# Summing the residual and the skip product in SBUF with an accumulating DMA, in a kernel that adds a state-space layer and a gated feed-forward layer

## The chip, the cores and the metric

The kernel runs on one core of one Trainium2 chip. The metric is device time in microseconds of one execution; the median of three runs of the kernel before is 177.08 us (176.98 to 179.34). The engines of the core are named as in the profile: PE (matrix products), DVE (vector), ACT (scalar), POOL (GpSimd) and SP, whose queue issues most DMAs.

## The reference

The input x has 2048 rows of 512 features. It is normalized once (xn), and three things are added to x: a diagonal complex state-space layer over the 2048 rows, a skip product xn * Dskip, and a GELU-gated feed-forward layer with 1376 hidden features.

```python
def _A_ref(x, Lambda_re, Lambda_im, B_re, B_im, C_re, C_im, log_dt, Dskip):
    ...
    Bu = jnp.einsum("bld,pd->blp", x + 0j, B_bar)
    for t in range(L):
        h = Lam_bar[None, :] * h + Bu[:, t, :]
        hs.append(h)
    hseq = jnp.stack(hs, 1)
    return 2.0 * jnp.einsum("blp,dp->bld", hseq, Cmat).real + x * Dskip[None, None, :]

def _B_ref(x, w_gate, w_up, w_down):
    return (_gelu(x @ w_gate) * (x @ w_up)) @ w_down

xn = _layernorm(x, axis=-1)
return x + _A_ref(xn, ...) + _B_ref(xn, ...)
```

The normalization of a row, (x - mean) / sqrt(var + eps), has no learned scale. All tensors are bfloat16, and so is the output.

## The kernel before

The 2048 rows are cut into four blocks of 512 rows, and each block into four tiles of 128 rows, so that there are 16 tiles. X holds all 16 input tiles in SBUF. XN holds normalized tiles in a ring of eight: tile tt lies in slot tt % 8, so block 2 overwrites the slots of block 0, and block 3 those of block 1. XD holds the 16 skip products.

For a block b the stages are these.

- LN(b) computes statistics (DVE, L614 and L615), a root on POOL (L621) and the normalized tiles (DVE, L633). For block 3 this is LN_act(3): mean and sum of squares on ACT (L652, L654), which also writes its by-product into the XN slots, then the root (POOL, L658) and the normalized tiles (DVE, L663).
- TR(b) transposes the four normalized tiles into XNT with four DMAs on SP's queue (L735).
- SKIP(b) multiplies each normalized tile with Dskip into XD, four products on DVE (L670).
- GU(b) multiplies with the gate and up weights (PE, L842), eleven tiles of hidden features. ACT evacuates the gate with the GELU (L857) and the up product (L861), DVE multiplies them (L863). The eleventh, of 96 features, goes another way (L816, L823, L825, L826) and needs a transposing DMA on SP (L828). For block 0 the first seven are computed in another way at the start of the kernel (L700, L711), and H0_T transposes them by DMA (L729).
- BU(b) is the input product of the state-space layer (PE, L748; evacuated by ACT, L757). CHAIN(b) is its recurrence on DVE: a rotation (L773 to L779), eight scans (L786), a carry for the next block and a rotation back (L798 to L802). scale_C scales the output matrix once (ACT, L591; DVE, L594).
- DN(b) forms the output of each tile in one PSUM bank. seed(j) writes X into the bank (ACT, L875); hidden(j) adds the eleven products with w_down, states(j) the eight products of the state-space layer (PE, L883, none of which starts a new sum); store(j) adds XD on DVE while it evacuates the bank into OUTB (L901), and a DMA on SP writes it out (L903). In blocks 0 and 1 all four hidden parts come ahead of the four states parts. Block 3 is the tail: its last tile is cut in columns, 384 and 128, in two banks.

PSUM has eight banks, which are taken in a ring in the order of the program. A tile of GU takes two, the eleventh tile two, a unit of BU one, DN four (the tail one more).

The order of the work comes from a planner inside the kernel. The program states its operations in a sequence with their reads and writes. PE and SP keep that sequence. On DVE, ACT and POOL the planner orders by due time: it goes back from the operations that need a result, with assumed durations, and picks, of what is ready, what is due first, filling gaps with later work. For a DMA it assumes 2 us plus its bytes at 350 bytes per ns. The order is fixed when the program is built, so on the chip an engine that waits for one operation also holds up all that stand behind it. Waits are semaphores, one for each DMA and one for each engine.

The sequence around the change, from the main part of build():

```python
CHAIN(1)
LN(2); SKIP(2)
TR(2)
load_C()
late_loads()
scale_C()
GU(1, [0, 1, 2, 10, 3, 4, 5, 6, 7, 8, 9])
BU(2)
CHAIN(2)
DN(0, True)
LN_act(3); SKIP(3)
GU(2, [0, 1, 2, 10, 3, 4, 5, 6, 7]); TR(3); GU(2, [8, 9])
```

Of the kernel before, what the change touches and what calls it, by code (L numbers as in the profile page):

```python
# [9 lines left out]
ALU = mybir.AluOpType  # L10
ACTF = mybir.ActivationFunctionType
BF16, F32, I32 = dt.bfloat16, dt.float32, dt.int32
# [333 lines left out]
L, D, P, F = 2048, 512, 512, 1376  # L346
NT, NB, KD, KP, KF = 16, 4, 4, 4, 11
# [17 lines left out]
def build(nc, ins, out):  # L365
    with ExitStack() as es:
        E = es.enter_context
        S = Sched(nc, es)
        ARENA_BYTES = 207 * 1024
        arena_t = E(nc.sbuf_tensor("arena", [128, ARENA_BYTES // 2], BF16))  # L370
        A = Arena(arena_t, ARENA_BYTES)
        PS = [E(nc.psum_tensor("PS%d" % i, [128, 512], F32)) for i in range(8)]
        BANK = [Buf("bank%d" % i, "ps", i, i + 1) for i in range(8)]

        def ring(parent, name, n):
            return [A.sub(parent, "%s%d" % (name, i), i) for i in range(n)]
# [10 lines left out]
        WDc = [Buf("WDc%d" % i, "sbx", 200 + 10 * i, 201 + 10 * i) for i in range(2)]  # L387
        XNT_all = A.alloc("XNT", [NB, KD, TB_], BF16)
        XNT = ring(XNT_all, "XNT", NB)
        X_all = A.alloc("X", [NT, D], BF16)  # L390
        X = ring(X_all, "X", NT)
        XN_all = A.alloc("XN", [8, D], BF16)
        XN = ring(XN_all, "XN", 8)
        DSKB = A.alloc("DSKB", [D], BF16)
        XD_all = A.alloc("XD", [NT, D], BF16); XD = ring(XD_all, "XD", NT)
        IDN = A.alloc("IDN", [128], BF16)
        BBT_all = A.alloc("BBT", [2, KD, P], BF16)
        BBT = [[A.sub(A.sub(BBT_all, "BBTc%d" % c, c), "BBT%d_%d" % (c, k), k) for k in range(KD)] for c in range(2)]
# [1 line left out]
        CT = [[A.sub(A.sub(CT_all, "CTc%d" % c, c), "CT%d_%d" % (c, s), s) for s in range(KP)] for c in range(2)]  # L400
# [57 lines left out]
        HTt = [[A.sub(HT[k], "HT%d_%d" % (k, ft), ft) for ft in range(KF)] for k in range(2)]  # L458
        SSs = [[A.sub(SSb[k], "SS%d_%d" % (k, s), s) for s in range(KP)] for k in range(3)]
# [4 lines left out]
        V = lambda fn, dur, r, w, tag="", after=(): S.op("vector", fn, dur, r, w, tag, after)  # L464
        ACT = lambda fn, dur, r, w, tag="", after=(): S.op("scalar", fn, dur, r, w, tag, after)
        POOL = lambda fn, dur, r, w, tag="", after=(): S.op("gpsimd", fn, dur, r, w, tag, after)
        PE = lambda fn, dur, r, w, tag="": S.op("tensor", fn, dur, r, w, tag)
# [70 lines left out]
        def load_C():  # L538
            load_T(CRAW, ("A_C_re", "A_C_im"))
# [85 lines left out]
        def recip(qb, rq):  # L625
            return V(lambda e: e.reciprocal(rq.ap, qb.ap), 150, [qb], [rq], "rq")
# [11 lines left out]
        def LN(b, js=range(4)):  # L638
            for j in js:
                stats(b, j)  # L640
            _, mn, qb, rq = root(b, js[0], js[-1] + 1)
            recip(qb, rq)
            norms(b, js, mn, rq, js[0])
# [4 lines left out]
        def LN_act(b):  # L648
            for j in range(4):
                tt = 4 * b + j  # L650
                xs = XN[tt % 8]
                ACT(lambda e, j=j, tt=tt, xs=xs: e.activation(xs.ap, X[tt].ap, ACTF.Copy, scale=-1.0 / D, accum_out=NMBs[j].ap),  # L652
                    d_act(512) + 190, [X[tt]], [xs, NMBs[j]], "mean")
                ACT(lambda e, j=j, tt=tt, xs=xs: e.activation(xs.ap, X[tt].ap, ACTF.Square, bias=NMBs[j].ap, accum_out=SQBs[j].ap),  # L654
                    d_act(512) + 190, [X[tt], NMBs[j]], [xs, SQBs[j]], "sq")
            sbq, qb, rq = (cols(t, b, 0, 4) for t in (SBQ, QB, RQ))
            V(lambda e: e.tensor_scalar(sbq.ap, SQB.ap, 1.0 / D, EPS_BF16, ALU.mult, ALU.add), D_TINY, [SQB], [sbq], "sbq")
            POOL(lambda e: e.tensor_tensor(qb.ap, sbq.ap, HALF.ap, ALU.pow), 1100, [sbq, HALF], [qb], "pow")  # L658
            recip(qb, rq)
            last = None  # L660
            for j in range(4):
                tt = 4 * b + j
                last = S.order_behind(V(lambda e, j=j, tt=tt: e.tensor_scalar(  # L663
                    XN[tt % 8].ap, X[tt].ap, NMBs[j].ap, rq.ap[:, j:j + 1], ALU.add, ALU.mult),
                    d_dve_ts4x(512), [X[tt], NMBs[j], rq], [XN[tt % 8]], "ln_n"), last)

        def SKIP(b):
            for tt in range(4 * b, 4 * b + 4):
                xs = XN[tt % 8]
                V(lambda e, tt=tt, xs=xs: e.tensor_tensor(XD[tt].ap, xs.ap, DSKB.ap, ALU.mult),  # L670
                  d_dve_tt2x(512), [xs, DSKB], [XD[tt]], "skip")

        XCd = lambda j, k: XC_all.ap[:, k, 128 * j:128 * (j + 1)]

# [57 lines left out]
        def TR(b, js=range(4)):  # L732
            for j in js:
                tt = 4 * b + j
                S.dma(lambda e, b=b, j=j, tt=tt: e.dma_start_transpose(  # L735
                    XNT[b].ap[:, :, 128 * j:128 * (j + 1)], XN[tt % 8].ap),
                    1.6 * 128 * 1024, reads=[XN[tt % 8]], writes=[XTk[b][j]], tag="tr_x%d" % b, issue=1280.0)
# [129 lines left out]
        def DN(b, split=False, tail=None):  # L867
            k2, k3 = b % 2, b % 3
            banks = [next_bank() for _ in range(4)]
            xbank = next_bank() if tail else None  # L870

            def seed(j, c0=0, c1=D):
                tt, bank = 4 * b + j, banks[j]
                bank = banks[j] if c0 == 0 else xbank
                ACT(lambda e: e.activation(PS[bank][:, c0:c1], X[tt].ap[:, c0:c1], ACTF.Copy), d_act(c1 - c0), [X[tt]], [BANK[bank]], "seed")  # L875

            def mms(j, ops, last, rds, c0, c1):
                bank = banks[j] if c0 == 0 else xbank

                def f(e):  # L880
                    ins_ = None
                    for n, (l_, r_) in enumerate(ops):
                        ins_ = e.matmul(PS[bank][:, c0:c1], l_[:, 128 * j:128 * (j + 1)], r_[:, c0:c1], start=False,  # L883
                                        stop=last and n == len(ops) - 1, skip_group_check=True)
                    return ins_
                PE(f, d_pe([c1 - c0] * len(ops)), rds + [BANK[bank]], [BANK[bank]], "DN%d" % b)

            def hidden(j, c0=0, c1=D):
                ops = [(HTt[k2][ft].ap[0:FROWS[ft], :], WD.ap[0:FROWS[ft], ft, :]) for ft in range(KF)]
                mms(j, ops, False, [HTt[k2][ft] for ft in range(KF)] + WDc, c0, c1)  # L890

            def states(j, c0=0, c1=D):
                ops = [(SSc[k3][s][c].ap, CT[c][s].ap) for s in range(KP) for c in range(2)]
                mms(j, ops, True, [SSs[k3][s] for s in range(KP)] + [CT[c][s] for c in range(2) for s in range(KP)], c0, c1)

            def store(j, c0=0, c1=D):
                tt = 4 * b + j
                bank = banks[j] if c0 == 0 else xbank
                ko = tt % 4
                ob = OUTB[ko] if c1 - c0 == D else Buf("OUTBp%d" % c0, "sb", OUTB[ko].lo + 2 * c0, OUTB[ko].lo + 2 * c1)  # L900
                V(lambda e: e.tensor_tensor(OUTB[ko].ap[:, c0:c1], PS[bank][:, c0:c1], XD[tt].ap[:, c0:c1], ALU.add),  # L901
                  d_dve_1x(c1 - c0), [BANK[bank], XD[tt]], [ob], "evO")
                S.dma(lambda e: e.dma_start(out[0, 128 * tt:128 * (tt + 1), c0:c1], OUTB[ko].ap[:, c0:c1]),  # L903
                      256 * (c1 - c0), reads=[ob], is_output=True, tag="st_out")

            if split:
                for j in range(4):
                    seed(j); hidden(j)
                for j in range(4):
                    states(j); store(j)  # L910
            elif tail:
                for j in range(3):
                    seed(j); hidden(j)
                for j in range(3):
                    states(j); store(j)
                parts = ((0, tail), (tail, D))
                for c in parts:
                    seed(3, *c)
                for c in parts:
                    hidden(3, *c); states(3, *c); store(3, *c)  # L920
            else:
                for j in range(4):
                    seed(j); hidden(j); states(j); store(j)
# [106 lines left out]
        BU(1, 4)  # L1030
        coefs()
        CHAIN(1)
        LN(2); SKIP(2)
        TR(2)
        load_C()
        late_loads()
        scale_C()
        GU(1, [0, 1, 2, 10, 3, 4, 5, 6, 7, 8, 9])
        BU(2)
        CHAIN(2)  # L1040
        DN(0, True)
        LN_act(3); SKIP(3)
        GU(2, [0, 1, 2, 10, 3, 4, 5, 6, 7]); TR(3); GU(2, [8, 9])
        BU(3)
        CHAIN(3)
        DN(1, True)
# [60 lines left out]
```

## Time and profile before

| | us |
|---|---|
| median of the runs shown | 177.08 (176.98 to 179.34) |
| span of the profiled execution, first to last instruction | 175.8 |
| PE busy | 172.7 (98%) |
| DVE busy | 159.6 (91%) |
| ACT busy | 95.9 (55%) |
| POOL busy | 10.7 (6%) |

The profiled execution is told by its span, 175.8 us; what lies around the span in an unprofiled run is taken as the difference from the median, 1.3 us. The lines of the chain and of a timeline have the start in us, the duration in us, and then the engine, the line of the kernel and the operation with its count; a bracket at the end gives the idle time of the engine just before and what ended it. In the page's list of DMA issues the last number is the median time from issue to landing. A share of busy time is an average over the whole span: it does not tell where an engine was waited for.

### The profile page before, as it was taken

How to read it: one execution, taken by the hardware profiler on the slowest of the kernel's cores; microseconds unless marked ns; L12 is line 12 of the kernel's file. 1: busy time of each engine (PE TensorE's matmuls, PEld its weight loads, DVE VectorE, ACT ScalarE, POOL GpSimd, SP SyncE). 2: the span in 40 equal slices, each digit the busy share in tenths (PEclk: the TensorE clock that was granted, in tenths of full speed). 3: DMA queues.
4: the chain of work that ended last, by engine and by line, in shares of the span. 5: the costliest groups of instructions: out<-in, count | busy, mean ns of one | idle time of the engine just before them, and what ended most of it. 6: DMA issues, size and time to landing. Idle time of an engine off the chain costs nothing.

```text
span 175.8 us, 2521 instructions
## 1 busy us (share of the span) xinstructions
PE 172.7 (98%) x889; PEld 84.7 (48%) x889; DVE 159.6 (91%) x279; ACT 95.9 (55%) x187; POOL 10.7 (6%) x24
## 2 busy tenths in 40 slices
PE   8999999999999999999999999999999999999995
PEld 2545464845544444444644444444454444444453
DVE  5988999997989989889899999989999899999931
ACT  5476678999766898383576792000667960000000
POOL 3212120210000000002100000000000000000000
DMA  5898999794998000002025000002001000000221
GB/s 174 262 323 139 228 158 224 132 138 99 202 306 200 4 0 2 0 30 89 4 45 106 0 0 0 4 0 90 30 0 30 4 0 0 0 0 0 95 95 56
DMA packets 32421, 14.37 MB, mean 82 GB/s; under 512 B 23736, under 2 KB 32408, under 8 KB 32408
## 3 DMA queue, kind: packets, MB, share of 16 engines
q1 hardware_dynamic: 32096, 13.94, 35.1%
q10 hardware_dynamic: 312, 0.27, 0.5%
q8 instruction: 7, 0.11, 0.3%
q14 instruction: 6, 0.05, 0.1%
HBM read 6.46 MB, written 2.10 MB: 49 GB/s over the span
## 4 chain that ended last, share of the span: by engine, by line
PE 96%; DMA 2%; SPq 0%; DVE 0%; issue 0%
PE PS L883 37%; PE PS L842 32%; PE PS L748 16%; PE PS L711 4%; PE PS L816 3%; PE PS L700 3%; DMA arena<-in_B_w_up_dram 2%; PE PS L683 0%; SPq L487 0%; SPq L496 0%; DVE arena L901 0%
## 5 line engine op out<-in xcount | busy, mean ns | idle before, releaser
L883 PE MATMUL PS<-arena 128*128 128x512 bf16 (+3 forms) x323 | 66.2, 366 | 0.0
L842 PE MATMUL PS<-arena 128*128 128x512 bf16 x264 | 58.1, 379 | 0.0
L883 PEld LDWEIGHTS PS<-arena 128*128 128x128 bf16 (+1 forms) x323 | 30.8, 98 | 35.2
L842 PEld LDWEIGHTS PS<-arena 128*128 128x128 bf16 x264 | 25.8, 98 | 30.2
L786 DVE TENSOR_TENSOR_SCAN arena<-arena 128x512 bf16<-128x512 f32 x32 | 38.9, 1254 | 0.0
L857 ACT ACTIVATE arena<-PS 128x512 bf16<-128x512 f32 x33 | 19.8, 599 | 26.1 <-DVE arena L901 16.7
L748 PE MATMUL PS<-arena 128*128 128x512 bf16 (+1 forms) x144 | 28.2, 355 | 0.0
L861 ACT ACTIVATE arena<-PS 128x512 bf16<-128x512 f32 x33 | 19.8, 599 | 5.4 <-PE PS L842 5.4
L748 PEld LDWEIGHTS PS<-arena 128*128 128x128 bf16 x144 | 14.1, 98 | 13.3
L875 ACT ACTIVATE PS<-arena 128x512 f32<-128x512 bf16 (+2 forms) x17 | 9.6, 581 | 19.7 <-DVE arena L901 19.0
L757 ACT ACTIVATE arena<-PS 128x512 bf16<-128x512 f32 x32 | 17.5, 596 | 1.8 <-PE PS L748 1.8
L901 DVE TENSOR_TENSOR arena<-PS,arena 128x512 bf16<-128x512 f32 (+2 forms) x17 | 10.9, 652 | 6.4 <-PE PS L883 6.3
L863 DVE TENSOR_TENSOR arena<-arena 128x512 bf16<-128x512 bf16 x33 | 13.2, 416 | 2.3 <-ACT arena L861 2.2
L775 DVE TENSOR_TENSOR arena<-arena 128x4096 bf16<-128x4096 bf16 (+1 forms) x5 | 9.2, 1858 | 0.4 <-ACT arena L610 0.4
L798 DVE TENSOR_TENSOR arena<-arena 128x4096 bf16<-128x4096 bf16 x4 | 9.1, 2287 | 0.1
L773 DVE TENSOR_TENSOR arena<-arena 128x4096 bf16<-128x4096 bf16 (+1 forms) x5 | 9.2, 1858 | 0.0
L799 DVE TENSOR_TENSOR arena<-arena 128x4096 bf16<-128x4096 bf16 x4 | 9.1, 2284 | 0.0
L720 ACT ACTIVATE arena<-PS,arena 128x256 bf16<-128x256 f32 (+1 forms) x16 | 6.5, 450 | 4.1 <-PE PS L700 2.4
L614 DVE BATCH_NORM_STATS2 arena<-arena 128x6 f32<-128x512 bf16 x12 | 7.7, 681 | 0.0
L711 PE MATMUL PS<-arena 128*128 128x512 bf16 (+1 forms) x40 | 7.1, 336 | 0.0
L723 DVE SCALAR_TENSOR_TENSOR arena<-PS,arena 128x256 bf16<-128x256 f32 (+1 forms) x16 | 6.3, 443 | 0.7 <-PE PS L700 0.7
L700 PE MATMUL PS<-arena 128*128 128x512 bf16 (+1 forms) x30 | 6.1, 342 | 0.3 <-DMA arena<-in_B_w_up_dram 0.3
(95 smaller groups left out, 124.1 us busy)
## 6 DMA issues: line engine op xcount, KB each, us to landing
out_dram<-arena SPq DMA_DIRECT2D x15, 128.0 KB, 1.7
arena<-in_A_x_dram SPq DMA_DIRECT2D x3, 512.0 KB, 5.5
arena<-in_B_w_down_dram SPq DMA_DIRECT2D x1, 1280.0 KB, 7.4
arena<-in_B_w_gate_dram SPq DMA_DIRECT2D x4, 128.0 KB, 3.4
arena<-in_B_w_up_dram SPq DMA_DIRECT2D x4, 128.0 KB, 3.6
arena<-in_B_w_gate_dram SPq DMA_DIRECT2D x1, 480.0 KB, 6.6
arena<-in_B_w_up_dram SPq DMA_DIRECT2D x1, 480.0 KB, 7.4
arena<-arena SPq DMA_TRANSPOSE x25, 3.1
```

Source lines behind the costliest of these rows:

```text
L700: PE(lambda e: e.matmul(dst, XCd(j, k), WGU[:, ws[0]:ws[-1] + 1, k, f0:f1], start=first, stop=k == KD - 1, skip_group_check=True), d_pe([w ...
L711: ins_ = e.matmul(dst, XCd(j, k), WGU[:, :, k, f0:f1], start=(k == 0), stop=(k == KD - 1))
L748: ins_ = e.matmul(PS[bank][:, 128 * j0:128 * j1], BBT[c][dk].ap[:, 128 * s:128 * (s + 1)], XNT[b].ap[:, dk, 128 * j0:128 * j1], start=(dk ...
L757: GATE["evBu"] = ACT(lambda e, bank=bank, k3=k3, s=s, c=c: e.activation(SSc[k3][s][c].ap, PS[bank][:, :], ACTF.Copy), d_act(512), [BANK[ba ...
L786: V(lambda e, g=g, rb=rb, init=init: e.tensor_tensor_scan(g.ap, rb, g.ap, init, ALU.mult, ALU.add), d_dve_scan(512), [g, PA[RRr]] + ([CARc ...
L842: ins_ = e.matmul(PS[bank][0:m, c0:c1], W.ap[:, dk, 128 * ft:128 * ft + m], XNT[b].ap[:, dk, c0:c1], start=(dk == 0), stop=(dk == KD - 1))
L857: GATE["last_gelu"] = ACT(lambda e, bg=bg, kk=kk, m=m: e.activation(GG[kk].ap[0:m, :], PS[bg][0:m, :], ACTF.Gelu_apprx_tanh), d_act(512), ...
L861: ACT(lambda e, bu=bu, kk=kk, m=m: e.activation(UPB[kk].ap[0:m, :], PS[bu][0:m, :], ACTF.Copy), d_act(512), [BANK[bu]], [UPB[kk]], "evU")
L863: V(lambda e, kk=kk, m=m, ft=ft, k2=k2: e.tensor_tensor(HTt[k2][ft].ap[0:m, :], GG[kk].ap[0:m, :], UPB[kk].ap[0:m, :], ALU.mult), d_dve_tt ...
L875: ACT(lambda e: e.activation(PS[bank][:, c0:c1], X[tt].ap[:, c0:c1], ACTF.Copy), d_act(c1 - c0), [X[tt]], [BANK[bank]], "seed")
L883: ins_ = e.matmul(PS[bank][:, c0:c1], l_[:, 128 * j:128 * (j + 1)], r_[:, c0:c1], start=False, stop=last and n == len(ops) - 1, skip_group ...
L901: V(lambda e: e.tensor_tensor(OUTB[ko].ap[:, c0:c1], PS[bank][:, c0:c1], XD[tt].ap[:, c0:c1], ALU.add), d_dve_1x(c1 - c0), [BANK[bank], XD ...
```

## The change

The buffer XD goes away. SKIP(b) now multiplies in place, so that the XN slot holds the skip product, and then one DMA per block, on POOL's queue, adds the block's four XN slots (2048 elements in each partition) into X in SBUF. X then holds x + xn * Dskip. In blocks 0 to 2 ACT seeds the banks with this sum as before, and since nothing is left to add, ACT also evacuates them with a copy. In block 3 there are no seeds: the first product of hidden(j) starts the sum in the bank, and DVE adds X while it evacuates. SKIP(2) and SKIP(3) are stated behind TR(2) and TR(3), which read the same slots.

```diff
-        XD_all = A.alloc("XD", [NT, D], BF16); XD = ring(XD_all, "XD", NT)
...
         def SKIP(b):
             for tt in range(4 * b, 4 * b + 4):
                 xs = XN[tt % 8]
-                V(lambda e, tt=tt, xs=xs: e.tensor_tensor(XD[tt].ap, xs.ap, DSKB.ap, ALU.mult),
-                  d_dve_tt2x(512), [xs, DSKB], [XD[tt]], "skip")
+                V(lambda e, tt=tt, xs=xs: e.tensor_tensor(xs.ap, xs.ap, DSKB.ap, ALU.mult),
+                  d_dve_tt2x(512), [xs, DSKB], [xs], "skip")
+            n0 = (4 * b) % 8
+            S.dma(lambda e, b=b: e.dma_start(X_all.ap[:, 4 * b:4 * b + 4, :], XN_all.ap[:, n0:n0 + 4, :], accum_op=ALU.add),
+                  1024 * 1024, reads=XN[n0:n0 + 4] + X[4 * b:4 * b + 4], writes=X[4 * b:4 * b + 4], tag="acc_x", queue="gpsimd", issue=1200.0)
...
-            def seed(j, c0=0, c1=D):
+            def seed(j):
                 tt, bank = 4 * b + j, banks[j]
-                bank = banks[j] if c0 == 0 else xbank
-                ACT(lambda e: e.activation(PS[bank][:, c0:c1], X[tt].ap[:, c0:c1], ACTF.Copy), d_act(c1 - c0), [X[tt]], [BANK[bank]], "seed")
+                if not tail:
+                    ACT(lambda e: e.activation(PS[bank][:, :], X[tt].ap, ACTF.Copy), d_act(D), [X[tt]], [BANK[bank]], "seed")
...
-                        ins_ = e.matmul(PS[bank][:, c0:c1], l_[:, 128 * j:128 * (j + 1)], r_[:, c0:c1], start=False,
+                        ins_ = e.matmul(PS[bank][:, c0:c1], l_[:, 128 * j:128 * (j + 1)], r_[:, c0:c1], start=first and n == 0,
                                         stop=last and n == len(ops) - 1, skip_group_check=True)
...
-                mms(j, ops, False, [HTt[k2][ft] for ft in range(KF)] + WDc, c0, c1)
+                mms(j, ops, bool(tail), False, [HTt[k2][ft] for ft in range(KF)] + WDc, c0, c1)
...
-                V(lambda e: e.tensor_tensor(OUTB[ko].ap[:, c0:c1], PS[bank][:, c0:c1], XD[tt].ap[:, c0:c1], ALU.add),
-                  d_dve_1x(c1 - c0), [BANK[bank], XD[tt]], [ob], "evO")
+                if not tail:
+                    ACT(lambda e: e.activation(OUTB[ko].ap, PS[bank][:, :], ACTF.Copy), d_act(D), [BANK[bank]], [ob], "evO")
+                else:
+                    V(lambda e: e.tensor_tensor(OUTB[ko].ap[:, c0:c1], PS[bank][:, c0:c1], X[tt].ap[:, c0:c1], ALU.add),
+                      d_dve_1x(c1 - c0), [BANK[bank], X[tt]], [ob], "evO")
...
                 parts = ((0, tail), (tail, D))
-                for c in parts:
-                    seed(3, *c)
...
-        LN(2); SKIP(2)
+        LN(2)
         TR(2)
+        SKIP(2)
...
-        LN_act(3); SKIP(3)
-        GU(2, [0, 1, 2, 10, 3, 4, 5, 6, 7]); TR(3); GU(2, [8, 9])
+        LN_act(3)
+        GU(2, [0, 1, 2, 10, 3, 4, 5, 6, 7]); TR(3); SKIP(3); GU(2, [8, 9])
```

More of the change, by code (lines that the diff above doesn't have):

```diff
@@ L870, in DN, with mms @@
             xbank = next_bank() if tail else None
-            def seed(j, c0=0, c1=D):
+            def seed(j):
                 tt, bank = 4 * b + j, banks[j]
-                bank = banks[j] if c0 == 0 else xbank
-                ACT(lambda e: e.activation(PS[bank][:, c0:c1], X[tt].ap[:, c0:c1], ACTF.Copy), d_act(c1 - c0), [X[tt]], [BANK[bank]], "seed")
-            def mms(j, ops, last, rds, c0, c1):
+                if not tail:
+                    ACT(lambda e: e.activation(PS[bank][:, :], X[tt].ap, ACTF.Copy), d_act(D), [X[tt]], [BANK[bank]], "seed")
+            def mms(j, ops, first, last, rds, c0, c1):
                 bank = banks[j] if c0 == 0 else xbank
@@ L882, in f @@
                     for n, (l_, r_) in enumerate(ops):
-                        ins_ = e.matmul(PS[bank][:, c0:c1], l_[:, 128 * j:128 * (j + 1)], r_[:, c0:c1], start=False,
+                        ins_ = e.matmul(PS[bank][:, c0:c1], l_[:, 128 * j:128 * (j + 1)], r_[:, c0:c1], start=first and n == 0,
                                         stop=last and n == len(ops) - 1, skip_group_check=True)
                     return ins_
-                PE(f, d_pe([c1 - c0] * len(ops)), rds + [BANK[bank]], [BANK[bank]], "DN%d" % b)
+                PE(f, d_pe([c1 - c0] * len(ops)), rds + ([] if first else [BANK[bank]]), [BANK[bank]], "DN%d" % b)
             def hidden(j, c0=0, c1=D):
                 ops = [(HTt[k2][ft].ap[0:FROWS[ft], :], WD.ap[0:FROWS[ft], ft, :]) for ft in range(KF)]
-                mms(j, ops, False, [HTt[k2][ft] for ft in range(KF)] + WDc, c0, c1)
+                mms(j, ops, bool(tail), False, [HTt[k2][ft] for ft in range(KF)] + WDc, c0, c1)
             def states(j, c0=0, c1=D):
                 ops = [(SSc[k3][s][c].ap, CT[c][s].ap) for s in range(KP) for c in range(2)]
-                mms(j, ops, True, [SSs[k3][s] for s in range(KP)] + [CT[c][s] for c in range(2) for s in range(KP)], c0, c1)
+                mms(j, ops, False, True, [SSs[k3][s] for s in range(KP)] + [CT[c][s] for c in range(2) for s in range(KP)], c0, c1)
             def store(j, c0=0, c1=D):
```

## The prediction

> **What bounds the kernel now.** I read the page first (busy shares, then the chain that ended last), then the chain in order of time, then each engine's timeline around the changed lines.
>
> ```profile
> span 175.8 us, 2521 instructions
> PE 172.7 (98%) x889; PEld 84.7 (48%) x889; DVE 159.6 (91%) x279; ACT 95.9 (55%) x187; POOL 10.7 (6%) x24
> ```
>
> PE is busy for 98% of the span. The chain in order of time says where the rest is: PE starts at 5.43 us, after the first weights, and from there no piece is anything but PE until the last output.
>
> ```profile
> 63.96 16.42 PE PS L883 x76
> 80.38 5.18 PE PS L842 x24
> 85.56 1.32 PE PS L816 x16
> ...
> 98.97 6.91 PE PS L748 x32
> ...
> 140.88 32.91 PE PS L883 x171
> 173.79 0.02 issue
> 173.81 0.29 DVE arena L901
> ```
>
> So the time is 5.4 us of loading, 168.4 us of unbroken matmuls and about 2 us of last evacuation and store. The granted clock is 1.00 in every stretch. The change takes away no matmul. It can therefore gain next to nothing; it can only put a hole into PE's row. The question for each edit is which deadline of PE it moves, and how much room there is.
>
> Deadlines, from the chain: hidden(0) of block 0 at 63.96; its states after 44 matmuls of 216 ns, at 73.46; GU(2) (gate and up of block 2) at 80.38; its fourth feature tile at 86.88, which writes the banks of the first (eight banks in a ring, and the three tiles and the remainder before it use all eight); BU(3) at 98.97.
>
> **What the change removes.** Twelve evacuations on DVE (L901, 682 ns each, 8.2 us; nearer 7.6 us of its row, since they follow each other more closely), and five seeds on ACT in the last block (three of 0.60 us, 0.51 and 0.28). PE is the bound, and these gaps hide under it: worth 0. The last evacuation stays on DVE, now reading X for XD: 0.
>
> **What it adds.** Twelve evacuations on ACT, by the nearest row (L757, 128x512 from PSUM) 596 ns each, 7.2 us. ACT has the room: idle from 106.6 to 123.26 (beside DN(1)) and from 143.5 on (beside DN(2)). In DN(0) it is free from 78.4 to 81.28 and its four evacuations fall between 75.2 and 81: 0, as long as ACT is not waiting for something else there. Without that cover GU(2)'s own evacuations start late; this returns below. The skip product is done in place, same 416 ns: 0, but it must follow the transposes that read XN, all landed well before.
>
> Four accumulating DMAs on POOL's queue. Each adds two waits: seeds wait for it, and so does whatever next overwrites its XN half, since the ring has eight slots. For blocks 2 and 3 nobody overwrites it. The planner sorts by due time, so SKIP(2) goes ahead of the due time of the seeds (135.65) and SKIP(3) into DVE's freed time before the last block's evacuations (first at 166.56); eight evacuations before them, 5 us, have left DVE by then. Price 0; a delay of the fourth matters only past 173. Blocks 0 and 1 matter:
>
> ```profile
> 33.44 1.42 DVE L670 TENSOR_TENSOR arena<-arena 128x512 bf16<-128x512 bf16 x4
> 34.78 0.17 DVE L626 RECIPROCAL arena<-arena 128x4 f32<-128x4 bf16 x1
> 35.06 1.38 DVE L633 TENSOR_SCALAR arena<-arena 128x512 bf16<-128x512 bf16 x4
> ...
> 42.58 0.43 DVE L863 TENSOR_TENSOR arena<-arena 128x512 bf16<-128x512 bf16 x1 [1.01 <-ACT arena L861]
> ...
> 71.52 1.09 DVE L863 TENSOR_TENSOR arena<-arena 128x512 bf16<-128x512 bf16 x3
> 72.53 1.42 DVE L670 TENSOR_TENSOR arena<-arena 128x512 bf16<-128x512 bf16 x4
> ```
>
> The skips of block 0 (33.44) stand just ahead of block 2's normalization (35.06), which overwrites XN0 to 3. The skips of block 1 (72.53) stand just ahead of block 3's, which begins on ACT and overwrites XN4 to 7:
>
> ```profile
> 73.03 0.63 ACT L652 ACTIVATE arena<-arena 128x512 bf16<-128x512 bf16 x1 [3.31 <-issue]
> ...
> 77.61 0.71 ACT L654 ACTIVATE arena<-arena 128x512 bf16<-128x512 bf16 x1
> ```
>
> ACT waits 3.31 us and goes 0.5 us after the first skip begins: that is this overwrite. In the changed kernel a whole DMA stands in both places.
>
> **How long is the DMA?** No accumulating DMA and no POOL DMA is in the trace. It reads 512 KB twice and writes 512 KB. Nearest rows, issue to landing:
>
> ```profile
> arena<-in_A_x_dram SPq DMA_DIRECT2D x3, 512.0 KB, 5.5
> arena<-in_B_w_up_dram SPq DMA_DIRECT2D x1, 480.0 KB, 7.4
> ```
>
> Lower end 1.7 us (the 128 KB store, same page); below nothing is excluded, since a wait is added. Upper end 14.8 us (two such 7.4 us loads after each other, one per operand). I take 7.4 us, the slower of the rows nearest in size, as more bytes move than in either, and 0.9 us of POOL before it (its small instructions here last 0.56 to 1.91 us): L = 8.3 us from last skip to landing. By the Trainium skill, "DMA: Bandwidth & Descriptors", section "Anatomy of one DMA — SWDGE (gpsimd) path", a POOL DMA takes 2.0 us plus its bytes at 436 GB/s; counting both operands that is an estimate of 4.4 us, with which no wait below would reach PE and the sum would be 177.1. The trace is slower than that formula for plain loads (3.2 us against 5.5), though those shared the engines.
>
> **Block 0.** SKIP(0) is now more urgent than block 2's statistics (the planner's due time is earlier by the DMA it must feed) and moves up to 30.58, where the statistics begin: done at 32.0. Landing 32.0 + 8.3 = 40.3, the four normalizations (1.38) end at 41.7. The two pre_c products of CHAIN(0) fill the gap, but pre_s, before at 39.21, starts 2.5 us late. Of that the 1.01 us at 42.58 and four smaller gaps up to 65 (0.23, 0.17, 0.16, 0.43) absorb 2.0; CHAIN(0) and the scaling of C end at 72.0 for 71.5, before the deadline of 73.46: 0. Queued behind it on SP are the four transposes of block 2 (37.83 to 43.02; then to about 47), the C, w_down and x loads; block 2's transposes are needed at 57.06, w_down (landing at 55, then 59) at 63.96: 0. H0's transposes stand before them and don't wait.
>
> **Block 1.** SKIP(1) stays behind the scaling of C, which is more urgent: done at 71.5 + 1.4 + the 0.5 of above = 73.4. Landing at 81.7, for a start of 73.03 before. Behind ACT's wait are eight instructions (5.4 us by the timeline), the fourth evacuation (0.5), and then GU(2)'s evacuations. The first tile's gate bank is free 0.5 us after these, at 81.7 + 5.4 + 0.5 + 0.5 = 88.1, and PE wants it at 86.88: **PE waits 1.2 us**. After it ACT catches up (1.1 us a tile against PE's 1.73). The normalization's root and products follow on DVE and POOL (2.9 us to the first one, from 82.10 on the old timeline): 90.5, within the 92.5 by which block 3's transposes must be issued (now 90.74 to 95.9, 2.5 us to land, 1.8 us of room before 98.97). If the planner puts GU(2)'s evacuations ahead of the statistics, the wait moves to those transposes, with a similar size.
>
> **Sum.** Profiled span 175.8 + 1.2 = 177.0; 1.3 us lie outside the span when compared with the median of 177.08, so 178.3.
>
> **The rivals.**
>
> No hole: L of 7.4 us or less lands block 1's sum by 80.3, and 86.88 holds. Everything is then hidden: 177.1 (176.7 to 177.5). For it: 3.3 us of idle ACT and the page's rule above. A planner that finds a hole in DVE's row for SKIP(1) before 71.5 gives the same. Chance 0.26.
>
> Slower, by one mechanism: ACT standing at L652 for block 1's DMA while PE's banks fill. It decides from L = 9.5 on, since a later landing of block 0's DMA also pushes SKIP(1): at 9.5 block 0 costs DVE 3.7 - 2.0 = 1.7, block 1 lands at 72.9 + 1.7 + 9.5 = 84.1, and PE waits 3.6, so 180.7. At L = 11: 44.4 on DVE, 5.2 - 2.0 = 3.2, of which 1.3 already stop PE at 73.46; landing 87.1, wait 6.6 - 1.3 = 5.3 and 1.3: 183.7. At 14.8: 191. Against it: no load of this size took so long. For it: all operands pass the engines more than once, and block 0's DMA meets transposes (DMA share 0.82 from 28 to 44). Chance 0.34 in all, 0.12 of it above 185.5.
>
> Starved queue: POOL's root of four columns (L658) took 1.91 us at 82.34 beside DVE's products, and 1.11 us at 33.61 (L621). If POOL also stands while DVE runs one long product (2.28 us at 75.85), L is 10.6 and the time near 182.9; its 0.02 goes to the slower side. The Trainium skill, "SBUF — State Buffer", section "Who interferes with whom", says that descriptor writing is locked out by DVE's two-port modes, and infers that tensor_tensor doesn't hold the port that it needs; by that rule it would not happen beside these products. No run here shows a POOL DMA.
>
> The change doesn't do what it says: the evacuations move, but nothing waited for DVE; then the relief is real and worth nothing, as in the no-hole case. Faster by over 2% would need a shorter PE row or load phase; nothing here does that: 0.02.
>
> **Numbers.** Small wait, up to 3.5 us (forecast, 178.3): 0.34, and 0.02 for orders that I didn't foresee. No hole: 0.26. So within 2% 0.62, slower 0.36, faster 0.02; 2% (3.5 us) is about what a measurement can tell, as the three runs shown span 176.98 to 179.34. The range holds the first two and the slower case up to L = 11.9: 176.7 to 185.5.
>
> **What would show it.** PE's chain broken by ACT (L857) near 86 to 89, or by block 3's transposes near 98; ACT L652 starting near 81.7; DVE L633 of block 2 near 40; the DMA's landing time near 7.4. Wrong if the DMA lands later than 9.5 us after its skip, if the planner moves SKIP(1), or if POOL's first DMA brings a cost at the start.

## The result, and the profile after

The changed kernel takes 179.47 us, the median of 15 runs (178.88 to 181.22); the kernel before takes 177.15 us in the runs beside them. The ratio is 1.013, with a 95% interval of 1.010 to 1.016: slower by an amount that is certain, but under 2%. The forecast was 178.3 us with a range of 176.7 to 185.5. The time lies in the range, 1.2 us above the forecast: the medians differ by 2.3 us, where 1.2 were forecast. The profiled execution is one of the shorter runs (178.96 us); its span is 1.8 us longer than before, and the rest of the 2.3 us lies in the scatter of the runs and in the clock, which comes up below.

Lines of the page of the changed kernel that answer to those of before, with its group of products that had no idle time before, the new evacuations, and the new DMA:

```profile
span 177.6 us, 2502 instructions
...
PE 171.8 (97%) x874; PEld 84.3 (47%) x889; DVE 152.6 (86%) x267; ACT 99.2 (56%) x194; POOL 15.4 (9%) x28
...
PE 86%; DVE 6%; DMA 3%; POOL 1%; issue 1%; ACT 1%; SPq 0%; DVEq 0%; ACTq 0%
...
L750 PE MATMUL PS<-arena 128*128 128x512 bf16 (+1 forms) x142 | 28.1, 355 | 2.2 <-DMA arena<-arena 2.1
...
L904 ACT ACTIVATE arena<-PS 128x512 bf16<-128x512 f32 x12 | 7.2, 597 | 36.4 <-PE PS L885 36.4
...
L672 POOL DMA_DIRECT2D arena<-arena x4 | 3.7, 936 | 108.8 <-DVE arena L669 65.0
...
arena<-arena POOLq DMA_DIRECT2D x4, 512.0 KB, 4.7
```

DVE was relieved of 7.0 us (159.6 to 152.6) and the time went up. The fourth line tells where: PE stood 2.1 us ahead of the input products (L750), waiting for a DMA from SBUF to SBUF. The last line shows that the new DMA is quick, 4.7 us from issue to landing, so it need not be the DMA that PE waited for. The chain in order of time, around that place:

```profile
80.09 2.60 PE PS L844 x12
82.77 0.60 ACT arena L859
...
87.78 3.55 DVE arena L788 x3
91.39 0.08 issue
91.48 2.10 POOL arena L657
93.60 0.19 DVE arena L625
93.88 1.38 DVE arena L662 x4
...
98.19 2.48 DMA arena<-arena
100.67 0.14 issue
100.80 7.07 PE PS L750 x32
...
175.81 0.29 DVE arena L906
```

Before, this chain was PE from 5.43 us on without a break. Now it leaves PE at 82.69, after twelve products of GU(2), and comes back at 100.80. (PE itself goes on with GU(2) until 98.67.) On the way it runs over an evacuation and two statistics on ACT (L859, L651), DVE's scans (L788), POOL's root for block 3 (L657), the normalized tiles of block 3 (L662) and their transposes (the DMA at 98.19). The products that PE waits to begin at 100.80 are BU(3), which began at 98.97 before. GU(2) began at 80.09 instead of 80.38, because this execution started 0.4 us sooner; so the hole of 2.1 us shows as 1.8 us in the span (175.8 to 177.6).

Why block 3 is normalized so late is seen on ACT. Its timeline in the changed kernel (start, duration, operation, and in the bracket the idle time before with its releaser):

```profile
78.40 0.60 ACT L904 ACTIVATE arena<-PS 128x512 bf16<-128x512 f32 x1 [1.13 <-PE PS L885]
78.89 0.62 ACT L651 ACTIVATE arena<-arena 128x512 bf16<-128x512 bf16 x1
...
82.77 0.60 ACT L859 ACTIVATE arena<-PS 128x512 bf16<-128x512 f32 x1 [0.33 <-PE PS L844]
83.27 0.62 ACT L651 ACTIVATE arena<-arena 128x512 bf16<-128x512 bf16 x1
...
85.80 0.62 ACT L651 ACTIVATE arena<-arena 128x512 bf16<-128x512 bf16 x1
...
89.07 0.71 ACT L653 ACTIVATE arena<-arena 128x512 bf16<-128x512 bf16 x1
```

Before, the eight statistics of block 3 stood together on an idle ACT, from 73.03 to 78.41. Now they overwrite the XN slots of block 1 only after the new DMA has read them, and in the planner's order they stand between the evacuations of DN(0) (L904) and those of GU(2) (L859): the four means at 78.89, 80.62, 83.27 and 85.80, and the four squares behind the first half of the eleventh feature tile. The last ends at 89.87, which is 11.5 us later. The sum for the root (L656) then stands on DVE behind three scans that had begun at 87.69, and starts at 91.24:

```profile
87.69 3.63 DVE L788 TENSOR_TENSOR_SCAN arena<-arena 128x512 bf16<-128x512 f32 x3
91.24 0.14 DVE L656 TENSOR_SCALAR arena<-arena 128x4 bf16<-128x4 f32 x1
```

The root takes 2.09 us, and the transposes of block 3 are issued from 94.33 on instead of 90.74. SP's queue, first in the kernel before and then in the changed one:

```profile
90.74 5.20 SPq L735 DMA_TRANSPOSE arena<-arena  x4
```

```profile
91.63 1.20 SPq L830 DMA_TRANSPOSE arena<-arena  x1
94.33 5.13 SPq L737 DMA_TRANSPOSE arena<-arena  x4
```

That is 3.6 us later, and as GU(2) ran 0.3 us sooner, 3.9 us later against PE. About 1.8 us of that was room; the rest is the hole of 2.1 us.

### The profile page after: what moved, and what is told of

Its sections match the earlier page's. It is cut to its first block, busy times and chain, and to the rows that moved or that the text cites. A ratio compares the mean times of both kernels' runs of the same rounds, so it can differ in the third digit from the quotient of the medians.

```text
span 177.6 us, 2502 instructions
## 1 busy us (share of the span) xinstructions
PE 171.8 (97%) x874; PEld 84.3 (47%) x889; DVE 152.6 (86%) x267; ACT 99.2 (56%) x194; POOL 15.4 (9%) x28
## 4 chain that ended last, share of the span: by engine, by line
PE 86%; DVE 6%; DMA 3%; POOL 1%; issue 1%; ACT 1%; SPq 0%; DVEq 0%; ACTq 0%
PE PS L885 37%; PE PS L844 24%; PE PS L750 16%; PE PS L713 4%; DVE arena L788 3%; PE PS L702 3%; PE PS L818 2%; DMA arena<-in_B_w_up_dram 2%; DMA arena<-arena 1%; POOL arena L657 1%; DVE arena L800 1%; DVE arena L865 1%; DVE arena L662 1%; PE PS L685 0%; ACT arena L651 0%
## 5 line engine op out<-in xcount | busy, mean ns | idle before, releaser
L844 PE MATMUL PS<-arena 128*128 128x512 bf16 x257 | 57.1, 379 | 0.4
L788 DVE TENSOR_TENSOR_SCAN arena<-arena 128x512 bf16<-128x512 f32 x32 | 38.6, 1253 | 0.0
L750 PE MATMUL PS<-arena 128*128 128x512 bf16 (+1 forms) x142 | 28.1, 355 | 2.2 <-DMA arena<-arena 2.1
L904 ACT ACTIVATE arena<-PS 128x512 bf16<-128x512 f32 x12 | 7.2, 597 | 36.4 <-PE PS L885 36.4
L859 ACT ACTIVATE arena<-PS 128x512 bf16<-128x512 f32 x33 | 19.8, 600 | 8.7 <-PE PS L844 5.3
L863 ACT ACTIVATE arena<-PS 128x512 bf16<-128x512 f32 x33 | 19.7, 602 | 3.2 <-PE PS L844 3.1
L750 PEld LDWEIGHTS PS<-arena 128*128 128x128 bf16 x144 | 14.0, 98 | 15.7 <-ACT arena L863 2.6
L759 ACT ACTIVATE arena<-PS 128x512 bf16<-128x512 f32 x32 | 17.4, 596 | 3.4 <-PE PS L750 3.4
L906 DVE TENSOR_TENSOR arena<-PS,arena 128x512 bf16<-128x512 f32 (+2 forms) x5 | 2.9, 585 | 14.2 <-PE PS L885 14.2
L672 POOL DMA_DIRECT2D arena<-arena x4 | 3.7, 936 | 108.8 <-DVE arena L669 65.0
L877 ACT ACTIVATE PS<-arena 128x512 f32<-128x512 bf16 x12 | 7.2, 602 | 0.5
L713 PE MATMUL PS<-arena 128*128 128x512 bf16 (+1 forms) x40 | 7.1, 337 | 0.0
```

What stands on the lines that cost most here:

```text
L713: ins_ = e.matmul(dst, XCd(j, k), WGU[:, :, k, f0:f1], start=(k == 0), stop=(k == KD - 1))
L750: ins_ = e.matmul(PS[bank][:, 128 * j0:128 * j1], BBT[c][dk].ap[:, 128 * s:128 * (s + 1)], XNT[b].ap[:, dk, 128 * j0:128 * j1], start=(dk ...
L759: GATE["evBu"] = ACT(lambda e, bank=bank, k3=k3, s=s, c=c: e.activation(SSc[k3][s][c].ap, PS[bank][:, :], ACTF.Copy), d_act(512), [BANK[ba ...
L788: V(lambda e, g=g, rb=rb, init=init: e.tensor_tensor_scan(g.ap, rb, g.ap, init, ALU.mult, ALU.add), d_dve_scan(512), [g, PA[RRr]] + ([CARc ...
L844: ins_ = e.matmul(PS[bank][0:m, c0:c1], W.ap[:, dk, 128 * ft:128 * ft + m], XNT[b].ap[:, dk, c0:c1], start=(dk == 0), stop=(dk == KD - 1))
L859: GATE["last_gelu"] = ACT(lambda e, bg=bg, kk=kk, m=m: e.activation(GG[kk].ap[0:m, :], PS[bg][0:m, :], ACTF.Gelu_apprx_tanh), d_act(512), ...
```

## The experiments

Three theories stood at the beginning. A: the order. The statistics lost the idle slot of ACT, the planner put them among GU(2)'s evacuations, and this order alone makes the root late. B: the DMA. Block 1's sum lands late, and an earlier landing would bring the time back. C: the crowd. The twelve evacuations that moved to ACT hold the statistics up.

**The statistics write elsewhere.** Their by-product, which nobody reads, goes into four tiles of its own, so that they wait for neither the skip products nor the DMA.

```diff
+        JNK = ring(A.alloc("JNK", [4, D], BF16), "JNK", 4)
...
         def LN_act(b):
-                xs = XN[tt % 8]
+                xs = JNK[j]
```

> The changed kernel, except that the by-product of block 3's statistics on ACT goes into four tiles of its own, so that ACT no longer waits there for block 1's accumulating DMA; the planner plans anew. Theory A (late order: what makes PE wait 2.1 us ahead of BU(3) is that the statistics can't start before the DMA and are then ordered between the evacuations of GU(2)): the statistics run near 70 to 78 us, the transposes of block 3 start near 90.5 instead of 94.3, PE has no hole, 177.1 us, ratio 1.00. Theory B (the landing of the DMA by itself sets the hole): the same, 177.1. Theory C (twelve evacuations more on ACT crowd it): the hole stays above 1 us, 178.5 or more.

Measured 176.94 us, ratio 0.9975 (0.9947 to 1.0003), and PE's row is whole: BU(3) begins at 98.70, 18.6 us after GU(2), as in the kernel before. The statistics begin at 69.22, now even ahead of the last three skips of block 1 (72.35). The whole loss hangs on that one overwrite. This doesn't yet tell A from B, since it removes the wait and the late order at once.

**Only the order.** The DMAs and all waits stay; on ACT the statistics go together ahead of GU(2)'s evacuations, and on DVE the root's sum goes behind four scans and the first tiles of block 3 ahead of the rest.

```diff
         S.schedule()
...
+        act[n:n] = stats[:2] + [evo[3]] + stats[2:]
...
+        dve[n0:n1] = (scan[:4] + tag("sbq") + h[:1] + scan[4:5] + h[1:2] + tag("rq") + tag("ln_n") + h[2:] + scan[5:])
         S.emit()
```

> The changed kernel with the same DMAs and waits, only the order within two engines is rewritten after the planning: on ACT the eight statistics of block 3 stand together behind the third evacuation of block 0, ahead of the evacuations of GU(2); on DVE the start of the root stands behind the fourth scan instead of the seventh, the normalized tiles ahead of the last three scans. Theory A: the statistics end near 85 instead of 89.9, the transposes of block 3 start near 91.5, PE's hole shrinks from 2.1 to 0.3 us or less, 177.1 to 177.5 us, ratio 1.00. Theory B: the DMA lands where it did, so the hole stays at 2.1 us, 179.4 us. Theory C: ACT does the same work in another order, so PE now stops at the fourth tile of GU(2) for over 0.5 us.

Measured 177.77 us, ratio 1.0032 (1.0002 to 1.0062). The statistics run from 79.58 to 85.44, and what is left of the hole has another releaser. PE in this kernel:

```profile
99.64 7.07 PE L750 MATMUL PS<-arena 128*128 128x512 bf16 x32 [0.28 <-ACT arena L859]
```

With the same DMAs and the same waits, 1.85 of the 2.13 us are gone. The 0.28 us that stay are a bank that ACT had not freed: a wait of the kind that was forecast, at a quarter of its size, but ahead of BU(3) and not in GU(2). The statistics hold up GU(2)'s evacuations, which start at 85.35 instead of 81.23, but ACT then also stands idle for 2.12 us before 90.47, until about the end of a product on DVE (90.39) that the new order had put behind the tiles of block 3. The edit rewrites two engines at once, and no run tells ACT's part in the 1.85 us from DVE's.

**Only the DMA.** The three skips of block 1 that stood behind the scaling of C go up to the first one, so that block 1's DMA is issued at 40.01 us and not at 73.30; ACT's order is unchanged.

```diff
         S.schedule()
+        sk = [o for o in dve if o.tag == "skip"][4:8]
+        dve[:] = [o for o in dve if o not in sk[1:]]
+        n = dve.index(sk[0]) + 1
+        dve[n:n] = sk[1:]
         S.emit()
```

> The changed kernel with the order of ACT as it is; on DVE the three late skip products of block 1 (71.65 us) move up to the first one (37.44 us), where DVE waits 1.6 us anyway, so that block 1's accumulating DMA is issued some 34 us earlier. Theory A: ACT's order is fixed, the statistics still stand between GU(2)'s evacuations, so the hole stays at 2.1 us (at least 1.5), 179 to 179.4 us, ratio 1.01. Theory B: the DMA lands before 50 us, the hole is gone, 177.1 us. Theory C: unchanged, 179.4.

Measured 180.38 us (four runs, 179.57 to 181.45), ratio 1.020 (1.014 to 1.026). A sum that lands some 30 us sooner gains nothing:

```profile
101.42 7.07 PE L750 MATMUL PS<-arena 128*128 128x512 bf16 x32 [2.14 <-DMA arena<-arena]
```

The hole is 2.14 us as before the edit: in this order the first statistic stands behind the third evacuation of block 0 (79.00), whenever the DMA lands. So B falls, and A holds: the DMA did its harm when the order was made, not when the kernel ran.

**The evacuations back on DVE,** as plain copies, with the due times of the first planning round, by which the changed kernel is planned too.

```diff
-                    ACT(lambda e: e.activation(OUTB[ko].ap, PS[bank][:, :], ACTF.Copy), d_act(D), [BANK[bank]], [ob], "evO")
+                    V(lambda e: e.tensor_copy(OUTB[ko].ap, PS[bank][:, :]), d_dve_1x(D), [BANK[bank]], [ob], "evO")
...
-        S.schedule()
+        S.schedule(1)
```

> The changed kernel with the twelve evacuations of blocks 0 to 2 back on DVE (a copy, no operand to add), planned by the due times that the changed kernel was planned by. Theory A: the statistics still wait for the DMA and still stand between GU(2)'s evacuations, two evacuations of 0.6 us fewer among them: hole 1 to 2.1 us, 178.3 to 179.4 us. Theory B: hole 2.1 us, 179.4. Theory C: ACT is relieved, hole below 0.3, 177.1.

Measured 178.27 us, ratio 1.0063 (1.0038 to 1.0088), and the hole is 0.89 us. ACT and PE in this kernel:

```profile
78.35 0.63 ACT L651 ACTIVATE arena<-arena 128x512 bf16<-128x512 bf16 x1 [8.63 <-DMA arena<-arena]
```

```profile
99.98 7.07 PE L750 MATMUL PS<-arena 128*128 128x512 bf16 x32 [0.89 <-DMA arena<-arena]
```

The first line is the only place in these runs where ACT is seen standing at the new DMA: idle for 8.63 us, released 4.6 us after the issue at 73.72. In the changed kernel ACT had evacuations to do until then. The statistics are spread as before and end at about 89.7, but two scans, not three, now stand ahead of the root's sum, which starts at 90.58 instead of 91.24, and the root takes 1.92 us instead of 2.09. These are 0.8 us; PE's row runs 0.4 us later in this execution, so that against PE it is 1.2 us. So the move of the evacuations is 1.2 of the 2.1 us. C has a part, though not through ACT's time: through the place that the planner gave to the root's sum on DVE.

**A ring of 16.** XN gets 16 slots, so that no normalization overwrites a slot that a DMA reads.

```diff
-        XN_all = A.alloc("XN", [8, D], BF16)
-        XN = ring(XN_all, "XN", 8)
+        XN_all = A.alloc("XN", [NT, D], BF16)
+        XN = ring(XN_all, "XN", NT)
```

> The changed kernel with sixteen XN slots instead of eight, so that nothing overwrites what an accumulating DMA reads: neither block 3's statistics nor block 2's normalization waits. Theories A and B: no hole ahead of BU(3), and DVE's 1.6 us of waiting near 38 to 39 us are gone as well; since PE is the bound and that wait is absorbed, no better than with the statistics alone set free: 177.1 us, ratio 1.00. If the wait near 39 us did cost PE something, this run is faster than the one with the statistics' own buffer. Theory C: 178.5 or more.

Measured 176.93 us, ratio 0.9988 (0.9973 to 1.0003), no hole. The wait of block 2's normalization, which is there in the changed kernel, is gone here, and nothing more is gained than with the four tiles above. The line of the changed kernel on DVE:

```profile
39.43 1.38 DVE L632 TENSOR_SCALAR arena<-arena 128x512 bf16<-128x512 bf16 x4 [1.59 <-DMA arena<-arena]
```

So these 1.59 us of DVE cost nothing.

**The kernel before, with the late order.** It has no accumulating DMA at all; only the places of the statistics on ACT and of the root and tiles on DVE are made like those of the changed kernel.

```diff
         S.schedule()
...
+        act[n:n + 10] = mean[:2] + ev[:3] + mean[2:3] + ev[3:6] + mean[3:] + ev[6:8] + sq + ev[8:]
...
+        dve[n0:n1] = scan[:1] + h[:1] + scan[1:4] + [sbq] + scan[4:6] + [rq] + norm + h[1:] + scan[6:]
         S.emit()
```

> The kernel before, with no accumulating DMA at all, and only the order within ACT and DVE rewritten after the planning: block 3's statistics stand between the evacuations of GU(2) as they do in the changed kernel, and the root and the normalized tiles correspondingly later. Theory A: statistics end near 89, the transposes of block 3 start near 94, PE waits about 2 us ahead of BU(3), 178.5 to 179.5 us, ratio 1.01. Theories B and C: no DMA and no evacuation was added, 177.1 us.

Measured 184.4 us, ratio 1.040 (1.036 to 1.044). An order of this kind makes a hole without any DMA, as A says. It is not the changed kernel's order to the letter, as DVE still evacuates here and fewer scans come ahead of the root's sum, and the size was missed twice. First, the hole is 5.18 us, not about 2: the three scans ahead of the root's sum stood behind a product of the eleventh tile at 91.11, so the sum starts only at 94.83. Second, there is a cost that no theory had. The chain and, below it, stretches of the timeline of this kernel (start and end; length; busy time of PE, PEld, DVE, ACT, POOL with their instructions; granted clock; DMA share; GB/s):

```profile
104.30 0.14 issue
104.44 8.75 PE PS L748 x32
```

```profile
99.26:104.44 5.18, 0.00 (x1) 0.03 (x2) 4.62 (x6) 4.03 (x8) 0.00 (x0) 1.00 0.48 98
104.44:108.00 3.56, 3.56 (x9) 1.27 (x10) 3.56 (x6) 1.29 (x3) 0.00 (x0) 0.52 0.00 0
108.00:113.19 5.19, 5.19 (x25) 2.33 (x24) 5.16 (x7) 4.87 (x9) 0.00 (x0) 1.00 0.00 0
```

The same 32 products take 8.75 us instead of 7.07: the granted clock is 0.52 for 3.6 us after the hole. A hole in PE's row can cost more than its length. Span: 5.18 + 1.68 = 6.9 of the 7.3 us by which it grew; GU(2) started 0.3 later.

**How long a hole drops the clock, and why the root is slow.** Three of the 15 runs of the changed kernel show a mean granted clock of 0.99 and take 180.76 to 181.22 us, 1.5 to 2.0 us more than the median of the others, 179.25 (one run at 1.00 took 180.38, so some scatter is not the clock's). Two of the four runs with the early DMA show it too, and none of the 46 runs of the four kernels whose hole is at most 0.9 us (own tiles, with the repeat below; 16 slots; the order alone; evacuations on DVE). Two kernels make the hole longer by putting the root's sum (L656) later on DVE.

```diff
         S.schedule()
...
+        dve[n0:n1 + 5 + 0] = between + tail + [sbq] + norm
         S.emit()
```

Here `between` is the product and the scan that followed the sum, and `tail` is empty.

> The changed kernel with one edit of order on DVE: the sum for the root of block 3 (L656) goes behind the product and the scan that now follow it, so that it starts at about 92.8 us instead of 91.24, and POOL's root then runs beside an idle DVE. Two questions. Is POOL's root slow because DVE scans beside it? If so, it takes about 1.1 us there (2.09 in the changed kernel, 1.03 to 1.11 at other places), ends 0.5 us later than before, and the hole ahead of block 3's input product is about 2.6 us, span 178.1. If the root takes 2.1 us wherever it stands at this point, the hole is 3.5 us, span 179.1. And how long a hole drops the clock? Holes of 2.1 us have gone with a granted clock of 0.99 in 5 of 19 runs, one of 5.2 us in 4 of 4. If length decides by chance of position, about a third to two thirds of these runs show 0.99, and each of them costs about 1.7 to 1.9 us more.

Measured 180.39 us (179.53 to 181.70), ratio 1.0185 (1.012 to 1.025), with a granted clock of 0.99 in the two slower of four runs. The sum moved from 91.24 to 92.95, 1.7 us later (0.4 of it because PE's row and all else ran that much later in this execution), and yet the hole grew by only 0.3 us, because the root was 1.06 us faster. POOL and PE in this kernel, against a root of 2.09 us at 91.48 in the changed one:

```profile
93.19 1.03 POOL L657 TENSOR_TENSOR arena<-arena 128x4 bf16<-128x4 bf16 x1 [18.60 <-DVE arena L656]
```

```profile
101.46 7.07 PE L750 MATMUL PS<-arena 128*128 128x512 bf16 x32 [2.43 <-DMA arena<-arena]
```

Beside an idle DVE the root of four columns takes 1.03 us. In the changed kernel a scan of 1.28 us began 0.02 us before it, and it took 2.09: 1.06 us more, a little less than the rest of the scan. In the kernel before, a product of 1.22 us began 0.17 us ahead of the root, and it took 1.91. In these runs it matters what DVE is doing when the root starts. In the kernel with only the order mended, a product began 0.24 us and a scan 0.58 us after the root, and the root was as fast as beside an idle DVE:

```profile
86.30 1.03 POOL L657 TENSOR_TENSOR arena<-arena 128x4 bf16<-128x4 bf16 x1 [11.38 <-DVE arena L656]
```

By the Trainium skill, "SBUF — State Buffer", section "Who interferes with whom", a DVE instruction with two inputs in SBUF contends with a GpSimd instruction that reads SBUF; the 1.91 and 2.09 us against 1.03 agree with that.

The second kernel puts three products of GU(2) ahead of the sum as well.

```diff
         S.schedule()
...
+        dve[n0:n1 + 5 + 3] = between + tail + [sbq] + norm
         S.emit()
```

> As the kernel with the root's sum behind one more scan, and three products of GU(2) on DVE (1.0 us) go ahead of the sum too: it starts at about 93.9 us. Hole about 3.6 us if the root takes 1.1 us beside a DVE that waits, 4.6 us if it takes 2.1. The clock should drop in more than half of the runs, all of them if a hole of 3.4 us or more is enough wherever it lies. By the Trainium skill, TensorE: Matmul & The Clock Gate, Part 1 (The HAM clock gate), the clock falls to half after about one idle window of 3.4 us, and the window runs freely: by that, holes of 2.1 us should never have dropped it. With the drop the time is about 179.4 + 1.5 + 1.8 = 182.7 us, without it 181.

Measured 183.88 us (183.81 to 184.91), ratio 1.037 (1.032 to 1.042). The hole is 4.37 us, between the two sizes expected: the root takes 1.03, but the third product waited 0.55 us for its operand, so that the sum starts at 94.74. All four runs show a clock of 0.98 or 0.99. Stretches of this kernel, columns as above:

```profile
98.90:101.30 2.40, 0.00 (x1) 0.00 (x0) 2.40 (x3) 0.96 (x2) 0.00 (x0) 1.00 0.54 109
101.30:103.27 1.97, 0.00 (x1) 0.03 (x1) 1.94 (x6) 0.13 (x1) 0.00 (x0) 0.51 0.33 67
103.27:108.00 4.73, 4.73 (x12) 1.66 (x13) 4.73 (x10) 2.29 (x4) 0.00 (x0) 0.50 0.00 0
```

The clock falls 2.4 us after PE's last product and stays down for about 6.7 us, into the work: BU(3) takes 9.48 us instead of 7.07. Hole and slow products, 4.37 + 2.41 = 6.8, are the growth of the span (175.8 to 182.5). The time is 1.2 us above the 182.7 expected with a drop, since the drop costs 2.4 us here and not 1.8, and the hole is longer than 3.6.

**The own tiles once more,** with more runs, to see whether the relief of DVE is worth anything.

> The changed kernel whose statistics of block 3 write their by-product into four tiles of their own, once more and in more rounds: the ratio was 0.9975 (0.9947 to 1.0003). If relief of DVE is worth something after all, the interval now ends below 1. If PE alone sets the time, as every theory here says, the ratio is 1.00 within 0.2%, and no version of this change beats the kernel before.

Measured 177.06 us, ratio 0.998 (0.9955 to 1.0005). The interval holds 1 again. No version here is shown to beat the kernel before. The three runs with the hole closed all lie slightly below 1, so a gain of a few tenths of a us is not excluded, but none of them alone tells it from zero.

## Why the prediction was wrong by a little, point by point

**What bounds the kernel: right.** The change could only put a hole into PE's row, and it did; the relief of DVE is worth next to nothing, as the three runs without a hole show (ratios 0.9975, 0.998 and 0.9988, all with 1 in the interval). The five seeds fall under the same head.

**The twelve evacuations on ACT at nothing: wrong in one place.** Their duration was right (597 ns for 596), and in DN(1) and DN(2) they are hidden. In DN(0) the condition "as long as ACT is not waiting for something else there" was weighed as time on ACT. What they did was to change the planned order, and with that the scans ahead of the root's sum: 1.2 us of the hole, by the run that moves them back.

**The length of the DMA: too long where it mattered.** L, from the last skip to the landing, was taken as 8.3 us. At block 0 it is right: skips done at 31.37, issued at 31.99, 7.4 us to land beside the transposes, so 8.0, and the normalization starts at 39.43 (forecast: 40.3). At block 1, where only output tiles move beside it, issue to landing is 4.6 to 4.7 us. The last skip ends at 72.73, so L is about 5.2. The estimate of 4.4 us by the Trainium skill, "DMA: Bandwidth & Descriptors", section "Anatomy of one DMA — SWDGE (gpsimd) path", is near this 4.6; at block 0 the trace has 7.4.

**Block 0: right.** Wait of 1.59 us on DVE, absorbed; taking it away with 16 slots gains nothing.

**Block 1: the step that failed.** The step let ACT wait at L652 with "eight instructions (5.4 us by the timeline)" behind it in one piece, ahead of GU(2)'s evacuations, and put the wait at GU(2)'s fourth tile: 1.2 us at 86.88. By that step's own working, the measured L of 5.2 gives no wait at all: 72.7 + 5.2 + 5.4 + 0.5 + 0.5 = 84.3, before 86.88. The no-hole rival had the condition "L of 7.4 us or less", and that was met too; yet there is a hole. What failed is thus the path, and not only a size: both took the order on ACT from the trace of before. That order was the planner's answer to an idle slot before 78. Once the statistics could not start before the DMA, the slot was gone, due times decided, and the statistics went among GU(2)'s evacuations; with the wait taken away (own tiles, 16 slots) the planner puts them ahead again. The sentence at the end of the step names this case and the place ("the wait moves to those transposes"), but gives it no working, only "a similar size". Worked out, it has two terms that the step did not have. The statistics end at 89.87 and not at 87.6 (81.7 + 5.4 + 0.5), 2.3 us later, although the DMA landed sooner; and the root's sum stands behind three scans, 1.4 us from 89.87 to 91.24. Root and first tile were nearly right (3.1 us from 91.24 to the first transpose, for 2.9). Together the transposes come at 94.33 and not at 90.5, 3.8 us later. The step left 2.0 us between 90.5 and 92.5, which held, so that 1.8 us remain, and 0.3 more because GU(2) ran sooner: the hole of 2.1. The runs confirm it from both sides: order alone mended, 0.28 us of hole; DMA alone mended, 2.14.

**Blocks 2 and 3, and the starved queue: right.** No hole comes after BU(3), and block 1's DMA issue took 0.92 us at 73.30 although DVE's products and then a long one (2.28 us at 73.66) ran beside it; the four took 0.86 to 1.05. What suffers beside DVE is POOL's root, not its DMA.

**The sum.** Forecast 1.2 us of hole, measured 2.13 in the profile. That a small loss came, and inside the range, is in part luck: with the DMA as short as it was, the forecast's own path gives no hole, and the loss came by another path, whose size had not been worked out. Not in the sum at all was the clock: the seven runs that show 0.99 take 1.5 to 2.2 us more than the others of their kernels, and in the two profiles where the clock is seen to fall this costs 1.7 and 2.4 us besides the length of the hole. Slower by over 2% had a chance of 0.36 for a late DMA; what came was a small loss within 2%, from an order that the forecast had left at "similar size".

## What to carry to other kernels

When a change adds a dependency to a kernel whose order is planned, the old timeline no longer tells in what order the engine will work: ask which idle slot the dependent work used, what else is due there, and which engine queues the next step stands in. A DMA can do its harm in the plan and not on the chip; to tell the two apart, mend the order and the arrival separately. Ask the planner too: the length that it plans (`makespan`, known when the program is built) is 175.3 us for the kernel before, 177.2 for the changed one and 175.3 again with the own tiles. Before any run, then, the plan lost the 1.8 us by which the span grew (175.8 to 177.6); the forecast did not ask it. On a bound engine with an unbroken row a hole of two microseconds may also drop the clock (0.99 in 3 of 15 runs here), so its price is at least its length.

## What the runs showed of the hardware that was not expected

The clock. A hole in PE's row of 4.37 or 5.18 us came with a granted clock of 0.50 to 0.52 in the profiles of the two kernels, and the next 32 products took 9.48 or 8.75 us instead of 7.07; all eight runs of the two show a mean clock of 0.98 or 0.99. Holes of 2.1 to 2.4 us came with a clock of 0.99 in 7 of 23 runs; that the same half rate stands behind this number is likely, as these runs are 1.5 to 2.2 us longer than the others of their kernels and the profiled run with the hole of 5.18 us, where about 3.6 us at half rate are seen, has the same mean of 0.99; but no profile shows one of the seven. By the Trainium skill, "TensorE: Matmul & The Clock Gate", "Part 1: The HAM clock gate", the clock falls to half after about one idle window of 3.4 us that runs freely. The trace differs in one point: in the kernel with the hole of 4.37 us the clock fell 2.4 us after the last product, so a wholly idle window was not needed. The half rate lasted 3.6 us in the one kernel and about 6.7 in the other, one and two of these windows.

The accumulating DMA. 512 KB onto 512 KB within SBUF took 4.6 to 4.7 us from issue to landing in three places of the changed kernel, at one of them beside output tiles, and 7.4 us beside transposes. The issue took 0.86 to 1.05 us of POOL, about the forecast's 0.9, but lies within the time from issue to landing and does not come ahead of it.

POOL's root beside DVE: 1.03 us when DVE was idle at its start, 2.09 when a scan had just begun.
